# Local and global attention feeding a gated MLP on one core: early loads placed in the line, later return of buffers in the planner, a newly annealed order

## The chip, the cores and the metric

The kernel runs on one core of a Trainium2 chip. The metric is the time of one execution on the device in microseconds (us), as the median of several runs. Engines are named as the profile names them: PE is TensorE's matmul and PEld its weight load, DVE is VectorE, ACT is ScalarE, POOL is GpSimd, SP is SyncE, which here only issues DMA transfers.

## The reference, cut to what matters

There are 8 batches, 8 heads of 64 columns, 512 local and 32 global rows. Local rows attend to a band of 32 neighbours on each side and to the 32 global keys; global rows attend to all 544 keys. The result (576 rows by 512) goes through a gated layer:

```python
s_g = scale * np.matmul(q_g, k_all.transpose(0, 1, 3, 2));  out_g = np.matmul(sm(s_g), v_all)
s_ll = np.where(np.abs(pos[:, None] - pos[None, :]) <= 32, scale * q_l @ k_l.T, -1e9)
out_l = np.matmul(sm(np.concatenate([s_lg, s_ll], -1)), np.concatenate([v_g, v_l], 2))
x = concat(out_g, out_l)                              # [8, 576, 512]
gate = sigmoid(sum_k conv_w[k] * shifted(x, k))       # 5 taps, causal
out = ((gate * (x @ w_val)) @ w_out).astype(float32)
```

Four weight matrices arrive as 64-bit floats, and the kernel splits them into two 32-bit halves itself.

## The kernel before, in words

The work is cut into named steps. A unit `u` (0 to 31) is a pair of heads of a batch, so a batch has four units. For a unit the steps are, in their order of need: `s` (PE, banded scores into the PSUM tiles sx and sy), `mx0`, `mx1` written `mx{u}.0` and `mx{u}.1` (DVE, mask and maximum of a half, which read sx and sy), `exp` (ACT, into the SBUF tile pm), `t` (PE, transposes of pm), `tc` (ACT, copies into pts), `av` (PE, times the values), `norm` (DVE), `xt` (PE, transposes), `xc`, `xh` (ACT), `halo`, `xl` (DVE), and `tap` and `conv` (the gate's taps, on DVE; for the first three units on PE, as `pc` with diagonal matrices that ACT makes in `dg`). For each batch `gs`, `gmax`, `gexp`, `gt`, `gtc`, `gav`, `gnorm`, `gx`, `gxc` do the 32 global rows of all four units, in two halves (`gexp{b}.0` and `gexp{b}.1`). `gs` writes into sx and sy as well, the same two tiles that `s` uses: half 0 is read from sx, half 1 from sy.

When a batch has its units, the layer's steps follow: `sig` (ACT), `g1.b.e.t` (PE, three matmuls each), `gv` (DVE), `gh` (ACT), `gl` (DVE), `g2.b.r.e` (PE, three matmuls each), `ob` (ACT), `st` (ACT, a store). The key `g` instead of a batch stands for the 256 global rows together, which come last. `w{k}.s0` to `w{k}.s7` (DVE) and `w{k}.high` (ACT) split the eight weight pieces; `g1` needs w0 to w3, `g2.0.0.e` needs w4 to w7.

The order of the program is the string `ORDER`, found by annealing outside the kernel. `Plan.order` walks along it, and every engine gets its steps in that order, so each engine executes its own queue strictly in turn. The planner's numbers (costs, `LAG`, `PAIR`, rings of buffers with `take` and `give`) do not put a wait into the program; the real waits come from the tiles that are read and written. They decide which order the annealing thinks good, and how many filler matmuls (`pz`, on zeros) `keep_clock` puts in front of a PE step for which a gap of more than `KEEP` ns is reckoned.

Loads are issued by SP, in order. `transfer` ties each load to the last PE instruction that stands before it in the line, so that the load is issued only when that instruction has ended. The loads named in `FIRST` are issued before the line begins, and wait for nothing on PE; there `q2` is the queries and keys of unit 2, `m0` the mask, `w1` a weight piece and `v0` the values of unit 0.

## Time and profile before

| what | value |
|---|---|
| runs (median, lowest, highest) | 374.15, 373.26, 375.1 us |
| profiled execution: its own time | 373.46 us |
| profiled execution: span from the first to the last instruction | 371.7 us |
| PE busy | 358.6 us |
| DVE busy | 311.6 us |
| ACT busy | 266.8 us |

The profiled execution's own time is 1.8 us longer than its span. Matmuls are pipelined and overlap, so a busy PE also hides short waits.

### The profile page before, as it was taken

Reading aid. Unit: us, or ns where it says so; the run is one execution under the profiler, and the core shown is the slowest. Engines: PE = TensorE matmul, PEld = TensorE weight load, DVE = VectorE, ACT = ScalarE, POOL = GpSimd, SP = SyncE. Lnnn points to the kernel's source line nnn. Section 1 sums busy time; section 2 is a strip of 40 time slices with the busy share of each in tenths; the row PEclk is TensorE's granted clock in tenths of the full one; section 3 lists DMA queues with packets and bytes.
Section 4 is the critical chain, followed back from the end, with each engine's and each line's share of the span. In section 5 each row is a group of like instructions: output and inputs, shape, how many; then the busy total and the mean of one; then the engine's idle time right before and its main releaser. Section 6 shows DMA issues by size and latency. Waiting matters only on the chain.

```text
span 371.7 us, 14822 instructions
## 1 busy us (share of the span) xinstructions
PE 358.6 (96%) x6349; PEld 280.7 (76%) x6349; DVE 311.6 (84%) x1094; ACT 266.8 (72%) x628; POOL 0.9 (0%) x7
## 2 busy tenths in 40 slices
PE   8899999997999899999999999999999999999995
PEld 4665678766878687878878888788778788788894
DVE  4899999998999887998879988888599837986871
ACT  4977869965789488856796777988876696835231
POOL 0000000000000000000000000000000000000000
PEclk9999999999999999999999999999999999999999
DMA  8986886485265733775586244654564110030112
GB/s 289 398 336 198 300 329 195 140 305 188 79 210 239 245 125 119 264 298 177 185 303 239 92 129 176 259 203 160 181 226 156 43 45 30 2 113 31 53 47 72
DMA packets 17250, 66.74 MB, mean 180 GB/s; under 512 B 1952, under 2 KB 4000, under 8 KB 17184
## 3 DMA queue, kind: packets, MB, share of 16 engines
q1 hardware_dynamic: 12240, 57.12, 43.7%
q10 hardware_dynamic: 4944, 8.67, 6.4%
q8 instruction: 50, 0.82, 0.9%
q14 instruction: 16, 0.13, 0.1%
HBM read 56.87 MB, written 8.91 MB: 177 GB/s over the span
## 4 chain that ended last, share of the span: by engine, by line
PE 74%; DVE 19%; ACT 4%; issue 1%; ACTq 0%
PE pv L621 22%; PE po L643 21%; PE ax L514 7%; PE pt L503 6%; PE sx L478 5%; DVE pm L490 3%; PE ax L533 3%; DVE gate L572 2%; PE sy L478 2%; PE ag L446 2%; PE pvg L621 2%; PE pog L643 1%; ACT pm L497 1%; DVE wraw L294 1%; DVE xs L524 1%
## 5 line engine op out<-in xcount | busy, mean ns | idle before, releaser
L497 ACT ACTIVATE pm<-pm,mx 128x128 f32<-128x128 f32 x256 | 81.5, 397 | 14.5 <-DVE mx L490 14.3
L572 DVE SCALAR_TENSOR_TENSOR gate<-xc,cw,gate 128x512 f32<-128x512 f32 x116 | 85.8, 748 | 1.6
L621 PE MATMUL pv<-xh,wvh 128*128 128x512 f32 x128 | 54.7, 428 | 0.6 <-issue 0.6
L643 PE MATMUL po<-woh,gh 128*128 128x512 f32 x128 | 54.3, 424 | 0.0
L621 PE MATMUL pv<-xl,wvh 128*128 128x512 f32 x128 | 50.4, 394 | 0.0
L643 PE MATMUL po<-woh,gl 128*128 128x512 f32 x128 | 50.3, 393 | 0.0
L643 PE MATMUL po<-wol,gh 128*128 128x512 f32 x128 | 50.2, 392 | 0.1
L621 PE MATMUL pv<-xh,wvl 128*128 128x512 f32 x128 | 50.2, 392 | 0.0
L506 ACT COPY pts<-pt 128x512 f32<-128x512 f32 x64 | 36.2, 586 | 19.5 <-PE pt L503 19.3
L478 PE MATMUL sx<-qk 64*32 64x128 f32 x1024 | 38.2, 275 | 3.0 <-ACT pg L420 2.9
L478 PE MATMUL sy<-qk 64*32 64x128 f32 x1024 | 36.9, 275 | 1.1 <-issue 0.7
L514 PEld LDWEIGHTS ax<-v,pts 128*32 128x32 f32 x2048 | 30.7, 109 | 9.2 <-issue 2.8
L503 PE MATMUL pt<-ident,pm 128*128 128x128 f32 x256 | 37.2, 275 | 0.1
L478 PEld LDWEIGHTS sx<-qk 64*32 64x32 f32 x1024 | 28.9, 106 | 10.8 <-ACT pg L420 4.0
L503 PEld LDWEIGHTS pt<-ident,pm 128*128 128x128 f32 x256 | 29.9, 141 | 9.3 <-issue 3.0
L514 PE MATMUL ax<-v,pts 128*32 128x65 f32 x2048 | 35.8, 221 | 0.5 <-ACT xc L537 0.2
L490 DVE CUSTOM_DVE_ANT_0 pm<-sx,mask 128x128 f32<-128x128 f32 x128 | 29.4, 287 | 6.8 <-PE sx L478 6.6
L629 DVE TENSOR_TENSOR gv<-pv,gate 128x512 f32<-128x512 f32 x32 | 22.0, 688 | 8.9 <-PE pv L621 8.8
L649 ACT COPY ob<-po 128x512 f32<-128x512 f32 x32 | 18.7, 586 | 14.9 <-PE po L643 12.6
L490 DVE CUSTOM_DVE_ANT_0 pm<-sy,mask 128x128 f32<-128x128 f32 x128 | 29.4, 286 | 0.0
L537 ACT COPY xc<-ax 128x512 f32<-128x512 f32 x32 | 18.8, 588 | 14.5 <-DVE gate L572 6.0
L621 PEld LDWEIGHTS pv<-xh,wvh 128*128 128x128 f32 x128 | 24.1, 188 | 6.7 <-issue 2.1
(113 smaller groups left out, 660.1 us busy)
## 6 DMA issues: line engine op xcount, KB each, us to landing
v<-in_vw_dram SPq DMA_DIRECT2D x32, 975.0 KB, 5.6
qk<-in_qk_dram SPq DMA_DIRECT2D x32, 624.0 KB, 4.8
out_dram<-ob ACTq DMA_DIRECT2D x32, 256.0 KB, 2.3
wraw<-in_w_val_dram SPq DMA_DIRECT2D x4, 512.0 KB, 12.4
wraw<-in_w_out_dram SPq DMA_DIRECT2D x4, 512.0 KB, 4.8
mask<-in_mask_dram SPq DMA_DIRECT2D x1, 256.0 KB, 4.4
out_dram<-obg SPq DMA_DIRECT2D x4, 64.0 KB, 1.7
out_dram<-obg ACTq DMA_DIRECT2D x4, 64.0 KB, 2.0
```

Source lines behind the costliest of these rows:

```text
L478: on_pe(T.matmul((sx, sy)[h][32 * j:32 * j + 32, i, :], qkt[rows, 32 * m:32 * m + 32], qkt[rows, k0:k0 + P], start=True, stop=True))
L490: V.tensor_tensor_reduce(out=pm[:, h, i, :], in0=s[:, i, :], in1=mask[:, i, :], op0=ALU.add, op1=ALU.min, scale=-SCALE, scalar=3.0e38, acc ...
L497: A.activation(out=pm[:, h, i, :], in_=pm[:, h, i, :], func=AF.Exp, bias=mx[:, c:c + 1], scale=-1.0)
L503: on_pe(T.transpose(pt[:, i, :], pm[:, h, i, :], ident))
L506: A.copy(st[u]["pts"][:, h], st[u]["pt", h])
L514: on_pe(T.matmul(ax[32 * j:32 * j + 32, h, E1 * i:E1 * i + E1], pts[:, h, i, 32 * j:32 * j + 32], vt[:, block_win(4 * i + j), h, :], start ...
L537: A.copy(xc[:, KW - 1:], flat(u)[:, SL:])
L572: V.scalar_tensor_tensor(out=acc, in0=xc[:, k:k + SL], scalar=cw[:, u % NDT, k:k + 1], in1=acc, op0=ALU.mult, op1=ALU.add)
L621: on_pe(T.matmul(box["pv", e], w[:, e, t * P:t * P + P], x, start=(t == 0 and q == 0), stop=(t == NDT - 1 and q == 2)))
L629: V.tensor_tensor(out=box["gv", e], in0=box["pv", e], in1=gates[x0 + e], op=ALU.mult)
L643: on_pe(T.matmul(box["po", r], g[:, e, rs], w[:, e, :], start=(e == 0 and q == 0), stop=(e == NDT - 1 and q == 2)))
L649: A.copy(box["ob", r][:, :at], box["po", r][:, :at])
```

## The change

`FIRST` keeps only three loads: units 0 and 1 of the queries and keys, and the mask. The ten others become steps of the line (`wi0` to `wi3`, `iq2`, `iq3`, `iv0` to `iv3`), and so wait for the PE instruction before them. In the planner, sx and sy of the global scores count as free when both `gexp` halves are done (before: when half 1 is done), and pm counts as free when both `t` halves are done (before: when `tc{u}.1` is done). `KEEP` falls from 1500 to 900, the reckoned cost of `s0` and `s1` rises, and `ORDER` is a new line of the same steps, with the ten loads added.

```diff
 ORDER = """
-cw s0 mx0.0 exp0.0 mx0.1 w0.s0 w0.s1 exp0.1 s1 t0.1 t0.0 w0.s2 w0.s3 mx1.0 tc0.1 w0.s4 tc0.0 w0.s5 av0 mx1.1 dg0 w0.s6
+wi0 cw wi1 dg0 s0 mx0.0 mx0.1 w0.s0 exp0.0 w0.s1 iv0 s1 w0.s2 w1.s0 exp0.1 mx1.0 w1.s1 mx1.1 iq2 w0.s3 iv1 t0.1 t0.0
...
-FIRST = "q0 m0 q1 w0 q2 v0 q3 w1 v1 w2 v2 w3 v3"
+FIRST = "q0 m0 q1"
...
-KEEP = 1500
+KEEP = 900
...
+        elif ("w", k) not in first:
+            plan.add(f"wi{k}", "SP", 450, wraws[k], [f"wi{k - 1}"] if k % 2 and ("w", k - 1) not in first else [])
...
-    for u in range(NQ, NU):
-        plan.add(f"iq{u}", "SP", 450, lambda u=u: load_qk(u), [f"iq{u - 1}"] if u > NQ else [], take=[("qk", u)])
+    for u in range(NU):
+        if ("qk", u) not in first:
+            plan.add(f"iq{u}", "SP", 450, lambda u=u: load_qk(u), [f"iq{u - 1}"] if ("qk", u - 1) not in first else [],
+                     take=[("qk", u)])
...
+        if ("v", u) not in first:
+            plan.add(f"iv{u}", "SP", 450, lambda u=u: load_v(u), [f"iq{u}"] if ("qk", u) not in first else [],
+                     take=[("v", u)])
...
-                     give=[("pt", "gagb"[2 * h:2 * h + 2] + f"{b}")] + ([("s", f"g{b}")] if h else []))
+                     give=[("pt", "gagb"[2 * h:2 * h + 2] + f"{b}")])
...
+        plan.add(f"fs{b}", "FREE", 0, lambda: None, [f"gexp{b}.0", f"gexp{b}.1"], give=[("s", f"g{b}")])
...
-        plan.add(f"s{u}", "PE", 1000, lambda u=u: l_s(u), [f"lq{u}"] + ([f"s{u - 1}"] if u else []),
+        plan.add(f"s{u}", "PE", (1400, 1500)[u] if u < 2 else 1000, lambda u=u: l_s(u), [f"lq{u}"] + ([f"s{u - 1}"] if u else []),
...
-                     give=[("pt", (u, h))] + ([("pm", u)] if h else []))
+                     give=[("pt", (u, h))])
+        plan.add(f"fp{u}", "FREE", 0, lambda: None, [f"t{u}.0", f"t{u}.1"], give=[("pm", u)])
```

The first place is SP at the start of the program: the loads in the order in which they are issued. Before:

```order
L314 DMA qk0_79<-in_qk_dram 128x1248
L843 DMA mask_64<-in_mask_dram 128x512
L314 DMA qk1_82<-in_qk_dram 128x1248
L314 DMA wraw0_84<-in_w_val_dram 128x4x256
L314 DMA qk2_86<-in_qk_dram 128x1248
L314 DMA v0_88<-in_vw_dram 128x1950
L314 DMA qk3_90<-in_qk_dram 128x1248
```

With the change:

```order
L314 DMA qk_79<-in_qk_dram 128x1248
L850 DMA mask<-in_mask_dram 128x512
L314 DMA qk_82<-in_qk_dram 128x1248
L314 DMA wraw_96<-in_w_val_dram 128x4x256 x2
L314 DMA v_166<-in_vw_dram 128x1950
L314 DMA qk_227<-in_qk_dram 128x1248
```

Both pieces of the first weight pair now stand ahead of unit 0's values, and unit 2's queries and keys behind them; all from the weights on wait for PE.

The second place is ACT at the global scores of batch 2, whose exponentials (`pg`) read sx and sy; PE's step `s9` writes the same two tiles next. Before:

```order
L419 ACTIVATE pg2_1_1647<-gs2_2_1_1575,gm2_1_1633 128x160
L420 ACTIVATE pg2_1_1647<-gs1_2_sy_1573,gm2_1_1633 128x384
L565 CAST xh6_1692<-xc6_1593 128x512
L649 COPY ob0_2_1695<-po0_2_1564 128x512
L807 DMA out_0_dram<-ob0_1_1558 128x512
L419 ACTIVATE pg2_0_1718<-gs2_2_0_1574,gm2_0_1629 128x160
L420 ACTIVATE pg2_0_1718<-gs1_2_sx_1572,gm2_0_1629 128x384
```

With the change:

```order
L419 ACTIVATE pg2_0_1619<-gs2_2_0_1556,gm2_0_1608 128x160
L420 ACTIVATE pg2_0_1619<-gs1_2_sx_1554,gm2_0_1608 128x384
L565 CAST xh6_1622<-xc6_1552 128x512
L419 ACTIVATE pg2_1_1647<-gs2_2_1_1557,gm2_1_1613 128x160
L420 ACTIVATE pg2_1_1647<-gs1_2_sy_1555,gm2_1_1613 128x384
L814 DMA out_0_dram<-ob0_1_1617 128x512
```

Half 1 stood first in the queue and half 0 three rows behind it; in the string, `s9` stood between the two. Now both halves stand ahead of `s9`, with one cast between them. Batch 3 (`gexp3.1`, `s13`, `gexp3.0`) changes in the same way.

The third place is DVE at the last step of the last weight piece, `w7.s7` (the row that writes `wol` from `wraw7`), for which `g2.0.0.3` waits. Before:

```order
L294 SCALAR_TENSOR_TENSOR wraw7_1130<-wraw7_1130 128x512
L635 TENSOR_TENSOR gl0_1133<-gv0_2_1321,gh0_1132 128x512
L568 TENSOR_TENSOR xl4_1228<-xc4_1082,xh4_1227 128x512
L288 TENSOR_SCALAR wraw7_1130<-wa7_1222 128x512
L635 TENSOR_TENSOR gl0_1133<-gv0_3_1396,gh0_1132 128x512
L289 SCALAR_TENSOR_TENSOR wol_75<-wraw7_1130 128x512
```

With the change:

```order
L635 TENSOR_TENSOR gl0_1185<-gv0_3_1434,gh0_1184 128x512
L452 TENSOR_SCALAR gd1_1_1463<-ag1_1_1413 128x1
L521 TENSOR_SCALAR mx6_987<-ax6_1245 128x8
L522 RECIPROCAL mx6_987<-mx6_987 128x8
L524 TENSOR_TENSOR xs6_1469<-ax6_1245,mx6_987 128x512
L289 SCALAR_TENSOR_TENSOR wol_75<-wraw7_1066 128x512
```

Of the steps ahead of `w7.s7` on DVE all are the same in both lines, except that `norm6` (three rows) and `mx8.0` (eight rows, further up) now stand ahead of it, and `xl4` behind. On PE the steps ahead of `g2.0.0.3` are the same but for `xt6`, which is now ahead, and `t8.0` in the place of `t7.0`.

## Rows read from the trace of the kernel before

**Rows 1.** The page: busy time of each engine.
```profile
PE 358.6 (96%) x6349; PEld 280.7 (76%) x6349; DVE 311.6 (84%) x1094; ACT 266.8 (72%) x628; POOL 0.9 (0%) x7
```
**Rows 2.** Busy time by stretch, with the view's own column heads.
```profile
core 0: us, PE busy (x) PEld busy (x) DVE busy (x) ACT busy (x) POOL busy (x), PEclk, DMA share, GB/s
5.14:20.00 14.86, 12.90 (x292) 9.02 (x292) 12.93 (x71) 12.17 (x38) 0.00 (x0) 1.00 1.04 399
20.00:80.00 60.00, 58.49 (x1185) 42.00 (x1184) 58.78 (x223) 48.39 (x124) 0.00 (x0) 1.00 0.71 245
80.00:95.00 15.00, 12.95 (x314) 9.90 (x320) 13.66 (x43) 9.15 (x24) 0.00 (x0) 1.00 0.59 217
95.00:125.00 30.00, 30.00 (x575) 23.78 (x576) 29.01 (x103) 23.48 (x56) 0.00 (x0) 1.00 0.58 199
```
**Rows 3.** PE's timeline: start, duration, row [idle before, releaser].
```profile
1.45 3.78 PE L705 MATMUL pz<-zf 128*128 128x512 f32 x4 [1.45 <-DVE zf L844]
...
10.44 2.15 PE L705 MATMUL pz<-zr 128*128 128x512 f32 x7
12.73 1.11 PE L514 MATMUL ax<-v,pts 128*32 128x65 f32 x64
```
**Rows 4.** DVE's timeline at the start: its first weight step, and unit 2's maximum.
```profile
8.63 0.43 DVE L282 TENSOR_SCALAR wa<-wraw 128x512 int32<-128x512 int32 x1 [0.16 <-DMA wraw<-in_w_val_dram]
...
16.09 0.29 DVE L490 CUSTOM_DVE_ANT_0 pm<-sx,mask 128x128 f32<-128x128 f32 x1 [1.05 <-PE sx L478]
```
**Rows 5.** SP's loads: first weight piece, all qk, all v.
```profile
L314 SPq DMA_DIRECT2D wraw<-in_w_val_dram x1: 433/433/433, 2.1 to 2.1; - x1
DMA to landing us min/median/max: 6.5/6.5/6.5
...
L314 SPq DMA_DIRECT2D qk<-in_qk_dram x32: 327/328/1012, 0.7 to 266.1; - x32
...
DMA to landing us min/median/max: 3.6/4.8/11.8
...
L314 SPq DMA_DIRECT2D v<-in_vw_dram x32: 327/328/4680, 3.4 to 280.6; - x32
...
DMA to landing us min/median/max: 4.6/5.6/16.1
```
**Rows 6.** DVE's timeline: a norm, half a mx, an xl, and the last weight step.
```profile
62.13 0.17 DVE L521 TENSOR_SCALAR mx<-ax 128x8 f32<-128x8 f32 x1
...
63.18 0.28 DVE L490 CUSTOM_DVE_ANT_0 pm<-sy,mask 128x128 f32<-128x128 f32 x1
...
64.02 0.69 DVE L294 SCALAR_TENSOR_TENSOR wraw<-wraw 128x512 f32<-128x512 int32 x1
...
73.40 0.69 DVE L568 TENSOR_TENSOR xl<-xc,xh 128x512 fp32r<-128x512 f32 x1
74.00 0.43 DVE L288 TENSOR_SCALAR wraw<-wa 128x512 int32<-128x512 int32 x1
...
75.53 0.68 DVE L289 SCALAR_TENSOR_TENSOR wol<-wraw 128x512 fp32r<-128x512 f32 x1
```
**Rows 7.** PE's timeline around the first matmul that reads wol of the last weight piece.
```profile
75.16 0.63 PE L503 MATMUL pt<-ident,pm 128*128 128x128 f32 x4
...
76.27 0.50 PE L643 MATMUL po<-wol,gh 128*128 128x512 f32 x1
```
**Rows 8.** Timelines: PE at s9 and s13, ACT before s9.
```profile
88.97 0.29 PE L478 MATMUL sx<-qk 64*32 64x128 f32 x1 [1.87 <-ACT pg L420]
...
127.92 0.29 PE L478 MATMUL sx<-qk 64*32 64x128 f32 x1 [1.05 <-ACT pg L420]
...
88.31 0.60 ACT L420 ACTIVATE pg<-gs_sx,gm 128x384 f32<-128x384 f32 x1
```
**Rows 9.** PE's waits, whole span: total us, times, longest.
```profile
PE pv L621 <- issue: 0.6, 1, 0.6
PE gpt L429 <- DVE xg L454: 0.5, 1, 0.5
```

## The prediction

> **What bounds the kernel now.** I read the page first. PE is busy for nearly the whole span, DVE for five sixths of it, ACT for less [rows 1]. The new line holds the same computing steps, so PE's matmuls are the same but for the filler. Nothing can come out of PE's work; the time can only come from PE's waits, or go into new ones. So the question is where PE waits, and what it waits for.

> The windows by stretch answer the first half. From 95 us on PE is busy all the time. In the first 95 us it is not, and there the engine that is never free is DVE: from 5.14 to 20 us it is idle 14.86 - 12.93 = 1.9 us, from 20 to 80 us only 60 - 58.78 = 1.2 us [rows 2]. Beside the attention it splits eight weight pieces in that time. PE's queue runs in step with DVE's, and a step that is put earlier or later in DVE's queue moves the whole program. The place where this is read off is the last step of the last weight piece: DVE starts it at 75.53 us, it takes 0.68, so it ends at 76.21, and PE's first matmul on that half of the weights starts at 76.27 us [rows 6, 7]. After this, PE's own queue is the bound.

> The timelines around PE's longest gaps answer the other half. PE stands 1.87 us before s9 and 1.05 us before s13, both times released by ACT's exponential of the global scores [rows 8]. s9 writes the two PSUM tiles that the exponentials read; the planner took them for free after half 1, while half 0 was queued behind it on ACT. Two smaller gaps remain that are not at the start: 0.6 us before a pv matmul and 0.5 us before a gpt transpose [rows 9].

> **The change part by part.** *The accumulators of the global scores.* In the planner nothing is computed and no wait is added; what counts is that the new line puts both halves of gexp2 ahead of s9, and of gexp3 ahead of s13. The gaps of 1.87 and 1.05 us then go: -2.92 us. At most they go in full, at least nothing of them goes, if s9 then waits for another engine. I take the full value, because the exponential that released s9 began at 88.31 us and PE resumed at 88.97 [rows 8], with no other releaser in sight; how full DVE is there makes a rival below.

> *The probability tiles.* pm now counts as free when both transposes have read it, before: when the copy of half 1 was done. In neither trace row nor gap does a load or a score wait for pm by itself, so this costs and gives nothing at first hand; it only lets the annealing see what is true.

> *The early loads.* Ten loads leave the head of SP's queue and wait for PE. The first of them, a weight piece, now waits for the filler on zf, which ends at 1.45 + 3.78 = 5.23 us [rows 3], where it was issued at 2.1 us before and landed 6.5 us later, 8.6 us [rows 5]. Behind it in SP's queue stand the second weight piece, v0, the queries and keys of unit 2, and everything else, so a late start delays all of them, and DVE's weight steps wait for the first two, PE's av0 for the third. What does a load cost that is issued late? Before, the loads stood in a crowd: DMA engines full at 399 GB/s [rows 2], landings up to 11.8 us for qk and 16.1 us for v, where the quickest took 3.6 and 4.6 us [rows 5]. A weight piece of 512 KB is smaller than a qk load of 624 KB, so with three loads ahead instead of a crowd I estimate 4.0 us, between the quickest qk and the weight piece's own 6.5, and nearer to the first since only qk of unit 1 still moves when it is issued. It lands at 5.23 + 4.0 = 9.2 us. DVE is free for it at 8.63 - 0.16 = 8.47 us [rows 4], so it waits 0.8 us instead of 0.16, with bounds 0.3 (3.6 us) and 3.3 (6.5 us). v0, third in the queue, comes at about the same 12.7 us at which av0 starts now [rows 3], and the copies that av0 needs are no earlier. Against this, DVE's gap of 1.05 us before unit 2's maximum [rows 4] has work to fill it: in the new line norm0 and steps of two weight pieces stand there. Together DVE loses 0.8 us and gains 1.05 + 0.16 = 1.2: 0.4 us earlier by 20 us, with bounds of 0.9 earlier and 2.1 later.

> [...] The rows show early loads landing 11.8 and 16.1 us after their issue, because they queue behind each other, so what the early issue bought was a place in a full queue, and I go by the rows.

> *The filler.* Eleven filler rows of 0.31 us (seven take 2.15 [rows 3]) become four. They stand where PE waits anyway, so by themselves they cost nothing and give nothing. [...]

> *The new line up to w7.s7.* DVE now has norm6 and mx8.0 ahead of that step and xl4 behind it. norm: 63.18 - 62.13 = 1.05 us; half a mx: 64.02 - 63.18 = 0.84; xl: 74.00 - 73.40 = 0.60 [rows 6]. So +1.05 + 0.84 - 0.60 = +1.29 us on DVE; with the 0.4 from the start, w7.s7 ends 0.9 us later, at 77.1 us. PE in turn has one more step behind it at that point, xt6, four transposes, as long as the row that starts at 75.16 and ends with the next start, about 0.5 us [rows 7]. That is work done, not lost. Net, PE's queue is 0.4 us late here, with bounds of 0.1 early and 2.9 late. The steps after it on DVE (mx8.1, gmax2, norm7) are then as far ahead of PE as before.

> *The small gaps.* Of the 0.6 and 0.5 us [rows 9] I take half away, 0.5 us, since a new order keeps some gaps and makes others; bounds 0 and 1.1. Fewer table switches on ACT (the new queue has four loads of the table less) lie in ACT's idle time, which is a quarter of the span.

> *The sum.* -1.87 - 1.05 + 0.4 - 0.5 = -3.0 us. Against the profiled execution's own 373.46 us that gives 370.4 us; against the median of the runs, 374.15, which is 0.7 us more, 371.1 us. I predict the median: **371.1 us**. Over 0.5% (1.9 us) is about what a measurement of this kernel can tell from no change: faster begins below 372.3, slower above 376.0.

> **The rivals.** *DVE takes the wait over.* Once s9 no longer waits for ACT, PE runs into DVE, which is busy 13.66 of 15 us there and 29.01 of the next 30 [rows 2]. For it speaks that DVE's free time up to 125 us is only 1.3 + 1.0 us. Against it: of the 15 us, DVE is idle for 1.34, more than in the 60 us before. The price is the 1.87 us come back: 373.0 us, no change by measure. Chance 0.16.

> *The loads come late (slower).* Place: SP's queue at 5 to 20 us, where each load now follows a PE step. If they take what the first weight piece took, 6.5 us, although the crowd is gone, then DVE waits until 5.23 + 6.5 = 11.7 us, 2.5 us more than in the sum. The queries and keys of unit 3 are asked for only after unit 1's transposes and then come 2.5 us later too, and s3 waits; the weights of the next pair come behind. DVE loses 2.5 us about two times and more: 371.1 + 5.0 = 376.1 us, and each further late load adds to it. It decides from 4.9 us of lost DVE time on. For it: DVE has next to no free time up to 80 us, so each lost us counts. Against: the quickest loads in rows 5. Chance 0.08.

> *PE's clock falls at the start.* [...] The new line has less filler, and PE stands before t0, av0 and av1. The steps from s1 to s3 are some 6 us of matmuls by my estimate (an av is 1.11 us [rows 3], four transposes 0.5 [rows 7]). [...] Against it: the granted clock is 1.00 from 5.14 to 20 us, although PE was not always busy [rows 2]. Chance 0.06. [...]

> *All gaps go.* If the new line also keeps DVE free of its 1.9 us of early idle time and makes no new gaps, the sum is -2.92 - 1.1 + 0.4 - 1.9 = -5.5: 368.6 us. Chance 0.14.

> **How the numbers follow.** My own case has 0.56; its range is 369.4 to 372.9 (small gaps all gone and DVE early, or PE late by 2.2 us). Of it 0.48 lies below 372.3 and 0.08 above. Faster: 0.48 + 0.14 + 0.03 of the first rival = 0.65. Same: 0.08 + 0.13 + 0.06 = 0.27. Slower: 0.08. The range for 8 in 10 leaves out half of the slow rival and the ends of the others: 367.8 to 374.2.

> **What would show it.** Right: no gap before s9 and s13; the first weight step on DVE at about 9.2 us; the last weight step ending at about 77 us; PE without gaps from 95 us on; granted clock 1.00 at the start. Wrong: a first weight step after 11 us, DVE idle more than 4 us between 5 and 80 us, a PE gap of over 1 us released by DVE between 80 and 125 us, or new gaps where half a step is queued behind its user.

## The result, and the profile after

The changed kernel takes 375.29 us in the median of 20 runs (373.79 to 377.54), the kernel before in the same comparison 373.55 (372.69 to 375.1). The ratio is 1.0042, with a 95% interval of 1.0024 to 1.0059: 0.4% slower. That lies inside the 0.5% called no change, but the interval excludes no change, and 371.1 us and the gain were wrong. Below, medians are over all runs of a kernel and ratios leave disturbed runs out; where the two disagree the ratio counts.

The profiled execution took 377.54 us with a span of 375.8, 4.1 us more than the span before. It is the slowest of the 20, so its losses may be larger than those of the median run. First its page: busy time, then PE and the granted clock (PEclk) in 40 slices of 9.4 us, in tenths.

```profile
PE 360.2 (96%) x6342; PEld 282.1 (75%) x6342; DVE 311.4 (83%) x1094; ACT 262.4 (70%) x624; POOL 0.9 (0%) x7
...
PE   7688979999999999999999999999999999999995
...
PEclk9899998999999999999999999999999999999999
```

Then busy time by stretch, as in [rows 2], and six shorter stretches (same columns).

```profile
5.14:20.00 14.86, 10.65 (x280) 7.75 (x264) 11.15 (x58) 9.91 (x31) 0.00 (x0) 0.89 0.80 296
20.00:80.00 60.00, 54.83 (x1153) 38.51 (x1154) 54.63 (x212) 46.00 (x114) 0.00 (x0) 0.97 0.65 227
80.00:95.00 15.00, 15.00 (x224) 11.86 (x223) 14.58 (x47) 10.00 (x26) 0.00 (x0) 1.00 0.88 300
95.00:125.00 30.00, 30.00 (x670) 24.15 (x659) 28.04 (x110) 26.72 (x66) 0.00 (x0) 1.00 0.61 215
...
10.00:15.00 5.00, 2.07 (x37) 1.42 (x40) 4.84 (x25) 3.63 (x13) 0.00 (x0) 0.99 1.01 405
15.00:20.00 5.00, 4.94 (x125) 4.00 (x115) 3.21 (x12) 2.95 (x10) 0.00 (x0) 0.67 0.46 154
50.00:55.00 5.00, 3.09 (x69) 1.61 (x69) 4.93 (x25) 4.25 (x14) 0.00 (x0) 1.00 0.81 271
55.00:60.00 5.00, 4.77 (x19) 3.35 (x20) 4.11 (x13) 1.81 (x4) 0.00 (x0) 0.66 0.53 187
...
56.00:57.00 1.00, 1.00 (x3) 0.56 (x3) 0.94 (x4) 0.94 (x3) 0.00 (x0) 0.50 0.06 16
57.00:58.00 1.00, 1.00 (x3) 0.41 (x2) 0.95 (x3) 0.56 (x2) 0.00 (x0) 0.50 0.50 70
```

From 80 to 125 us PE has no gap: what stood before s9 and s13 [rows 8] is won. It is lost twice over ahead of 80 us. PE idles 14.86 - 10.65 = 4.21 us up to 20 us (before 1.96) and 5.17 from 20 to 80 (before 1.51) [rows 2]. And its work became slower: it is busy 1.6 us longer than before [rows 1] although seven filler rows (2.15 us [rows 3]) are gone, so the same matmuls took some 3.75 us more. Most of that is, by my estimate, the clock: granted at 1.00 in every window of the profiled execution before [rows 2], now two stretches of 3.4 us at 0.50 (14.90 to 18.32 and 55.87 to 59.28 us; last two rows), each behind a gap of PE's. Half of twice 3.4 us is 3.4 us, the most that I let them explain. The sum: +2.25 + 3.66 - 2.05 (80 to 125 us) - 1.05 (s13) + 3.75 - 2.15 = 4.4, against 4.1 us of span.

The timelines of DVE and PE name the places: the first weight piece and av0 as in [rows 3, 4], and the transposes t5.0 and t5.1, where [rows 3] has nothing to set beside.

```profile
9.85 0.43 DVE L282 TENSOR_SCALAR wa<-wraw 128x512 int32<-128x512 int32 x1 [1.54 <-DMA wraw<-in_w_val_dram]
...
11.16 0.47 PE L705 MATMUL pz<-zr 128*128 128x512 f32 x1
14.57 0.73 PE L514 MATMUL ax<-v,pts 128*32 128x65 f32 x28 [2.93 <-ACT pm L497]
...
52.81 0.27 PE L503 MATMUL pt<-ident,pm 128*128 128x128 f32 x1
55.23 1.19 PE L503 MATMUL pt<-ident,pm 128*128 128x128 f32 x7 [2.15 <-ACT pm L497]
```

PE's waits (total, times, longest), and from issue to landing of the first weight piece (issued at 5.04 us), of v0 (6.16 us), and of v0 in the kernel before (3.4 us).

```profile
PE ax L514 <- ACT pm L497: 2.9, 1, 2.9
PE pt L503 <- ACT pm L497: 2.5, 2, 2.1
PE ax L514 <- DMA v<-in_vw_dram: 2.0, 2, 1.8
...
DMA to landing us min/median/max: 4.8/4.8/4.8
...
DMA to landing us min/median/max: 8.3/8.3/8.3
...
DMA to landing us min/median/max: 9.2/9.2/9.2
```

The view puts av0's 2.93 us on an ACT exponential. But v0 lands at 14.44 us, 0.13 before PE goes on, so that wait is v0's; before, it landed at 12.60. The 2.0 us are waits for the third and fifth v. And t5.0's first transpose runs at 52.81, and ACT had ended unit 5's exponentials at 51.70, so the seven that start 2.15 us later are not held by them either; the rows of line 497 that end at 54.63 are unit 6's. What held PE here is the subject of half the experiments.

### The profile page after: what moved, and what is told of

Same layout as the page of the kernel before. It is cut to its first block, busy times and chain, and to the rows that moved or that the text cites. A ratio compares the mean times of both kernels' runs of the same rounds, so it can differ in the third digit from the quotient of the medians.

```text
span 375.8 us, 14813 instructions
## 1 busy us (share of the span) xinstructions
PE 360.2 (96%) x6342; PEld 282.1 (75%) x6342; DVE 311.4 (83%) x1094; ACT 262.4 (70%) x624; POOL 0.9 (0%) x7
## 4 chain that ended last, share of the span: by engine, by line
PE 87%; DMA 5%; DVE 4%; ACT 2%; issue 1%; SPq 0%; ACTq 0%
PE pv L621 24%; PE po L643 24%; PE ax L514 8%; PE pt L503 7%; PE sx L478 5%; DMA v<-in_vw_dram 4%; PE ax L533 3%; PE ag L446 3%; PE sy L478 2%; PE pc L597 2%; DMA wraw<-in_w_val_dram 2%; PE pvg L621 2%; PE pog L643 1%; PE gpt L426 1%; PE gs_sx L403 1%; ACT pm L497 1%
## 5 line engine op out<-in xcount | busy, mean ns | idle before, releaser
L497 ACT ACTIVATE pm<-pm,mx 128x128 f32<-128x128 f32 x256 | 80.3, 395 | 7.1 <-DVE mx L490 6.9
L503 PE MATMUL pt<-ident,pm 128*128 128x128 f32 x256 | 38.8, 280 | 2.5 <-ACT pm L497 2.5
L503 PEld LDWEIGHTS pt<-ident,pm 128*128 128x128 f32 x256 | 31.3, 144 | 11.6 <-ACT pm L497 4.2
L643 PEld LDWEIGHTS po<-woh,gh 128*128 128x128 f32 x128 | 24.1, 188 | 6.7 <-issue 1.8
```

What stands on the lines that cost most here:

```text
L497: A.activation(out=pm[:, h, i, :], in_=pm[:, h, i, :], func=AF.Exp, bias=mx[:, c:c + 1], scale=-1.0)
L503: on_pe(T.transpose(pt[:, i, :], pm[:, h, i, :], ident))
L643: on_pe(T.matmul(box["po", r], g[:, e, rs], w[:, e, :], start=(e == 0 and q == 0), stop=(e == NDT - 1 and q == 2)))
```

## The experiments

Four theories. **L**: the ten early loads wait for PE, come late, and PE waits for v. **C**: less filler lets PE's clock fall. **O**: the order of the early work loses by itself. **P**, added when the traces showed gaps without a fitting releaser: PE runs out of its own program, which comes in pieces while it runs. The page of the changed kernel lists a queue (q8 of the kind "instruction", first row: 50 packets, 0.82 MB, so 16 KB each), and the view of DMA from 52.7 to 53.95 us, over the gap at t5, has one of its packets (second row; the trace has it from 52.81 to 53.91). That these are PE's instructions is my inference, and what each holds an estimate from these counts: 0.82 MB over PE's 12,684 matmuls and weight loads is 65 bytes for each, and 12,684 over 50 packets is 254, or 127 matmuls with their loads.

```profile
q8 instruction: 50, 0.82, 0.9%
...
q8 instruction: 1, 0.02, 5.5%
```

**1. Loads free.** Changed line, loads issued at once.

```
-FIRST = "q0 m0 q1"
+FIRST = "q0 m0 q1 w0 w1 v0 q2 v1 q3 w2 w3 v2 v3"
-wi0 cw wi1 dg0 s0 mx0.0 ... iv0 s1 ... iq2 w0.s3 iv1 ... iq3 s2 ... wi2 ... wi3 s3 ... iv2 w3.s1 iv3
+cw dg0 s0 mx0.0 ... s1 ... w0.s3 ... s2 ... s3 ... w3.s1
```

> The changed kernel, with the ten early loads taken out of the line and issued at once before it, in the same sequence (w0 w1 v0 q2 v1 q3 w2 w3 v2 v3); the line of work and the four filler rows stay. Theory L (the loads that wait for PE arrive late, and DVE and PE wait for them): the first v lands near 12.6 us as in the kernel before instead of 14.44, DVE's waits for weight pieces (1.54 and 0.87) fall under 0.3, PE's wait for the third v (1.8) goes; about 4 us less than the changed kernel's 375.3, so 371 to 372. Theory C (PE's clock falls after its waits, since less filler stands there): the filler is the same, so the time follows the clock: over 374 if rows at the lower level remain. Theory O (the new order of the early work is itself worse): within 1 us of 375.3.

Measured 373.86 us, ratio 1.0002 (0.9979 to 1.0025). Every wait that L names went (v0 landed at 12.60), but only about 0.4% came back: more than O allows and less than L forecast. PE now stood in front of s3:

```profile
22.17 0.42 PE L478 MATMUL sx<-qk 64*32 64x128 f32 x1 [3.08 <-DVE wraw L288]
...
20.00:30.00 10.00, 7.83 (x86) 5.15 (x87) 6.99 (x30) 5.36 (x18) 0.00 (x0) 0.66 0.72 268
```

Scores read no weight, so the releaser named is only the last event; the fourth qk had landed at 19.11. The clock was 0.66 over the ten us from 20. This execution took 375.87 us, 2 us above the median of 1; it also waited 1.81 us for a v at 297.91 us, far behind the start.

**2. More filler.**

```
-                if not opened and gap > KEEP:
-                    keep_clock(int((gap - 400) * 0.55 / 235))
+                if t.name in {'s1': 4, 'av0': 7}:
+                    keep_clock({'s1': 4, 'av0': 7}[t.name])
```

> The changed kernel with the filler rows of the kernel before: 4 rows ahead of the second scores and 7 ahead of the first product with v, in place of 3 and 1. Theory C (the clock): the stretch at half clock after the first wait (3.4 us, up to 1.7 us of work lost) does not come, the mean clock is 0.995 or more, 373.6 to 374.2. Theories L (loads late) and O (order worse): the filler lies inside PE's wait of 2.9 us for the first v, and the time stays at 375.3 within 0.5.

Measured 377.31 us, ratio 1.0054 (1.0022 to 1.0086): nothing gained. The stretch at 0.50 behind av0 went, another came around a later wait, of 1.71 us for the fourth qk, at 22 us (the clock is 0.97 over the first 51.65 us, in a row further down). More filler removed one fall of the clock, and the time did not follow.

**3. The global exponentials alone.** Kernel before, two tasks moved.

```
-gexp2.1 conv5.2 g2.0.3.0 s9 ... gexp2.0 ... gexp3.1 ... s13 gexp3.0
+gexp2.1 gexp2.0 conv5.2 g2.0.3.0 s9 ... gexp3.1 gexp3.0 ... s13
```

> The kernel before with two tasks moved in its line: the late halves of the global exponentials of batches 2 and 3 stand directly behind the early halves, ahead of the local scores s9 and s13; nothing else changes. If the middle term of the prediction is right: PE's waits of 1.87 and 1.05 us behind them go, 2.9 us less than 373.55, 370.6 to 371.2. If another wait takes their place (DVE's or ScalarE's next task comes late by as much): 372.5 to 373.6.

Measured 371.54 us, ratio 0.9932 (0.9911 to 0.9953): 2.5 us won where 2.92 were forecast. The gap before s13 is gone, that before s9 has shrunk from 1.87 to this:

```profile
87.75 0.29 PE L478 MATMUL sx<-qk 64*32 64x128 f32 x1 [0.86 <-ACT pg L420]
```

**4. Hybrid.** The line and `FIRST` of the kernel before for 279 tasks (up to s8), then the remaining tasks in the changed line's order.

> The line of the kernel before for its first 279 tasks (up to s8, near 68 us; early loads and 11 filler rows as there), then the rest of the changed kernel's line. If the loss lies wholly in the start and the gain wholly behind it (theories L, C and O alike, against the rival that the changed line's later part loses too): 373.55 less the 3.9 us that the traces show as won behind the start, so 369.2 to 370.4. If the later part is no better by itself: 372.5 to 374.

Measured 370.89 us, ratio 0.9918 (0.9895 to 0.9940), clock 1.00, half a microsecond above the forecast. So the loss lies in the start (the changed start stands at 1.0042 with the same rest) and the gain behind it.

**5. Hybrid with the waits.** Ten loads put into the hybrid's line.

```
-FIRST = "q0 m0 q1 w0 q2 v0 q3 w1 v1 w2 v2 w3 v3"
+FIRST = "q0 m0 q1"
+wi0 wi1 cw s0 iv0 ... s1 iq2 iv1 ... s2 iq3 ... xt0 wi2 ... pc0.0 iv2 iv3 ... av1 wi3
```

> The hybrid of the fourth experiment (start of the kernel before, then the changed line; 370.89 us), with one edit: the ten early loads wait for PE at the changed kernel's places. Theory L (the waits themselves cost the start): the first v lands about 1.8 us later, and with the later weight pieces and v tiles it loses 1.5 to 3 us: 372.4 to 374. Theory O (the order of the early work is what loses): within 0.6 of 370.9.

Measured 375.34 us, ratio 1.0053 (1.0036 to 1.0069). The waits alone cost 4.4 us on the old order by the medians and 5.0 by the ratios, above L's own range. PE waited for v0 and then for the third qk, and its clock fell (0.89 from 5.14 to 20 us):

```profile
14.91 1.12 PE L514 MATMUL ax<-v,pts 128*32 128x65 f32 x64 [2.14 <-DMA v<-in_vw_dram]
16.99 0.39 PE L478 MATMUL sx<-qk 64*32 64x128 f32 x1 [0.96 <-DMA qk<-in_qk_dram]
```

**6. Two loads later.** Changed kernel, `iq7 iv5` moved to behind `t5.1`.

> The changed kernel (375.29 us) with two loads, q7 and v5 (issued at 46.63 and 48.35 us in its trace), moved behind the transposes t5.1, some 4 us later; all else stays. Theory P (PE stood still from 53.09 to 55.23 because the next 16 KB of its own program, fetched from 52.81 to 53.91, had stood behind these loads' packets): the fetch comes by 50 us, that gap goes, and with it the clock's fall behind it (1.3 us): 2 to 3.5 us less, 371.8 to 373.3. If the gap has another cause (ScalarE's exponentials, as the view of waits names it): the gap stays, 374.6 to 376.

Measured 376.40 us, ratio 1.0065 (1.0044 to 1.0086): a miss in time. The gap at t5 and the clock's fall behind it did go, the q8 packet coming at 50.45 in place of 52.81 us; but v5, now late itself, held av5 for 1.3 us, and in this execution PE waited 3.4 us for v0. The step was right and the trade bad.

**7 and 9. Hybrid up to s3.** The line before only for the first 22 us, without the third weight's pieces.

> The line of the kernel before only up to the scores s3 (near 22 us, without the pieces of the third weight), all early loads issued at once, and the changed line from there. If the changed order loses nothing by itself after 22 us (theory L: its loads came late there): within 0.7 of the hybrid, 370.6 to 371.6. If the order from 22 to 57 us loses by itself, or PE's program comes late there as in theory P: 373 to 375.5, with a PE gap of about 2 us near 50 us.

> As the run before it was meant, with the third weight now issued ahead of the fourth again: the line of the kernel before up to the scores s3 (near 22 us, without the third weight's pieces), all early loads issued at once, 11 filler rows, and the changed line from there. If the changed order loses nothing by itself behind 22 us: within 0.7 of the hybrid's 370.9. Theory P (PE's own program comes late near 50 us, where products with v, scores and short transposes stand close together) or O (the order from 22 to 57 us loses): 372.5 to 375, with a PE gap of about 2 us near 50 us for P.

The first, 379.15 us (ratio 1.0166), says nothing of the order: issued ahead of the third weight piece, the fourth goes into the buffer half of the second, which is then computed from wrong data, and DVE waited 4.30 us for it. In the second (w2 ahead of w3) the ratio is 1.0015 (0.9991 to 1.0040), 1% above the hybrid, with a gap inside s6 at 50.93 us of 1.75 us and one of 1.55 us for DVE at 34.56 us (0.67 in the hybrid), although its trace (373.22 us) is of its fastest execution. So the changed order from 22 to 57 us loses by itself, as P and O would have it.

**8. v0 ahead of the third qk** in the hybrid.

> The hybrid (370.89 us) with the first v issued ahead of the third qk, and 3 filler rows in place of 7 ahead of the first product with v. Its PE waited 2.26 us there for that v, which landed at 12.6: it should land near 11.0, and 1.0 to 1.6 us less come of it, 369.3 to 369.9. Rival: the third qk lands 2.4 us later (12.6 in place of 10.2) and scores s2 or ScalarE's copies take the wait over: 370.6 to 371.2.

Measured 371.29 us, ratio 0.9933 (0.9920 to 0.9946): the rival came true. The 2.26 us of the expectation were mostly filler: in the hybrid's trace the filler ends at 12.43 us and av0 starts at 12.73. Here v0 landed at 11.12 and av0 began at 11.40, but the third qk landed only at 12.69, and PE stood still three times before and inside s2, the longest 0.58 us at 14.63.

**10. Convolution earlier.** As 1, with `pc0.0 pc0.1` ahead of `av1`.

> The first experiment (changed line, early loads issued at once, 373.86 us) with two convolution steps, pc0.0 and pc0.1, moved ahead of the product with v av1, where the kernel before has them. In the first experiment PE stood still for 3.08 us ahead of the scores s3 with the piece of its program landing inside the gap, and its clock fell behind it. Theory P (the changed order takes up PE's program faster than the pieces come while the loads fill the queues; rows of 512 columns stretch it): the gap falls under 0.6 and the fall with its 2.8 us goes, 369.5 to 371.5. If the gap is a load's (the fourth qk): the gap stays, and 373.5 to 374.5.

Measured 373.67 us, ratio 0.9988 (0.9968 to 1.0009). PE waited 2.35 us for the halo, a DVE row of 0.06 us that stands behind steps of two weight pieces. This wait is of O's kind, and the run no test of P.

**11. Three loads free.** `FIRST = "q0 m0 q1 w0 w1 v0"`, seven loads left in the line.

> The changed kernel (375.29 us) with three of the ten early loads, w0, w1 and the first v, issued at once; the other seven wait in the line as before. Theory L: the first v lands at 12.6 in place of 14.44 and DVE's wait for the first weight goes, 1.5 to 2.5 us less; the wait of 1.78 for the third v stays: 372.8 to 373.8. If all ten must be free (PE's wait moves on to the fourth qk or the third v): 374.7 to 375.5.

Measured 373.20 us, ratio 0.9980 (0.9962 to 0.9999): 0.6% below the changed kernel, as L has it; 2.3 us of wait for the third v stayed, and 1.70 us stood before s3.

**12 and 13. Pairs parted.** As 9 with `pc2.2` between `av4` and `s6`; as 1 with `pc0.0 pc0.1` between `av1` and `s3`.

> The run of the hybrid up to s3 (375.91 us; PE gap of 1.75 us inside the scores s6, near 50 us) with one convolution step, pc2.2, moved from behind s6 to between the product with v av4 and s6. Theory P: four rows of 512 columns (0.9 us) give the piece of PE's program time to come; the gap falls to under 0.9 and 1 to 2 us come off: 374 to 375. If the gap is not of the program: it stays at 1.7 or moves whole, within 0.6 of 375.9.

> The first experiment (changed line, early loads at once, 373.86 us; PE gap of 3.08 us ahead of s3, clock fall of 6.8 us behind it) with the convolution steps pc0.0 and pc0.1 moved to between av1 and s3, where DVE's halo they need is ready. Theory P: the 1.9 us of convolution lie inside the wait, the gap falls to about 1.2, the fall is shorter or goes: 370.8 to 372.3. If the wait is one of s3's own operands: nothing is won, 373.3 to 374.5.

12: 374.41 us, ratio 1.0019 (0.9993 to 1.0046), by ratio no change from 9, though the gap fell from 1.75 to 0.87, by the 0.9 us of convolution put ahead of it. 13: 376.00 us, ratio 1.0060 (1.0036 to 1.0084), a miss by time, and the most telling one. The gap did not shrink and did not stay with s3; it now stood before pc0.0, whose halo (first row below) was there at 19.42:

```profile
19.36 0.06 DVE L542 MEMSET xc<- 128x4 f32 x1
...
22.04 0.59 PE L597 MATMUL pc<-xc,diag 128*128 128x512 f32 x1 [3.00 <-DVE wraw L288]
```

In these two runs it is the place in the program that counts, matmul 349, and not the task. The windows from the span's start to just before the gap count PE's matmuls. At s3 in 1 and at pc0.0 in 13:

```profile
0.00:22.15 22.15, 15.18 (x348) 9.65 (x348) 15.97 (x79) 15.71 (x44) 0.85 (x7) 0.98 0.95 350
...
0.00:22.00 22.00, 14.83 (x348) 9.56 (x349) 16.09 (x79) 15.71 (x44) 0.85 (x7) 1.00 0.95 349
```

And near 50 us, at t5 in the changed kernel, inside s6 in 2 and in 9 (both with seven filler rows more, so that the same count comes at an earlier task):

```profile
0.00:55.20 55.20, 44.40 (x984) 28.32 (x984) 45.49 (x203) 39.91 (x110) 0.85 (x7) 0.97 0.77 275
...
0.00:51.65 51.65, 43.64 (x984) 28.50 (x984) 41.94 (x182) 37.36 (x102) 0.85 (x7) 0.97 0.80 280
...
0.00:50.90 50.90, 43.45 (x984) 27.22 (x984) 42.59 (x182) 37.35 (x102) 0.85 (x7) 1.00 0.79 284
```

In each of these, PE starts its next matmul a nearly fixed time, 1.28 to 1.45 us, after the end of the q8 packet that the trace shows there. In the table the larger differences belong to places without such a wait (no gap there is over 0.4 us):

| kernel | matmul 349: packet ends, starts | matmul 985: packet ends, starts |
|---|---|---|
| before | 20.20, 21.45 (+1.25) | 47.93, 54.30 (+6.4) |
| hybrid (4) | 19.30, 20.98 (+1.68) | 47.74, 54.02 (+6.3) |
| changed | 17.93, 22.14 (+4.2) | 53.91, 55.23 (+1.32) |
| 1, loads free | 20.73, 22.17 (+1.45) | 52.65, 53.94 (+1.29) |
| 2, more filler | 18.01, 20.07 (+2.1) | 50.40, 51.68 (+1.28) |
| 9, hybrid to s3 | 19.45, 21.03 (+1.58) | 49.61, 50.93 (+1.32) |
| 13, pair parted | 20.68, 22.04 (+1.37) | 55.05, 56.35 (+1.31) |

**14. Repaired.** As 11, with both partings and v2, v3 issued earlier.

> The run with three free loads (373.2 us) with three edits: pc0.0 and pc0.1 between av1 and s3, pc2.2 between av4 and s6, and the third and fourth v issued directly behind the fourth and fifth weight pieces, before their old places. Theories L and P together: PE's gaps of 1.70 (ahead of s3) and 2.29 us (for the third v) go, and the clock's fall behind the second: 3.5 to 4.5 us less, 368.7 to 369.9. If DVE's order is what remains (theory O): a wait for a maximum, a halo or a weight piece takes their place, 371.5 to 373.

Measured 375.53 us, ratio 1.0041 (1.0018 to 1.0063): neither. The wait for the third v went, and at matmul 985 no gap was left; but at matmul 349 PE stood 2.46 us in front of pc0.0, and its clock was at 0.66 from 20 to 30 us. As in 13, the task moved to that count stood still there.

One piece of the estimated 127 ahead of matmul 349 stands matmul 222 (349 - 127). There the kernel before itself has a gap, inside s2, for which the view names no releaser ("issue"):

```profile
14.93 0.30 PE L478 MATMUL sy<-qk 64*32 64x128 f32 x2 [0.73 <-issue]
```

The first q8 packet ends at 13.51, 1.42 us earlier. Gaps of 0.28 to 0.80 us stand at matmul 222 in 3, 4, 7, 8, 9, 12 and 15 too, 1.22 to 1.45 us behind that packet. So, if P holds, it already cost the old order a little, and in 8, where matmul 222 came at 14.63 us (14.48 in the hybrid), it helped to take back what the earlier v0 had won.

**15. Hybrid with less filler.** As 4, with 3 and 1 rows.

> The hybrid (370.89 us, 11 filler rows, no stretch at half clock) with the filler of the changed kernel: 3 and 1 rows. Theory C (less filler alone lets PE's clock fall, since PE then stands idle for 2 us ahead of the first product with v): a fall of 3.4 us near 12 to 17 us and 1 to 1.7 us more, 371.9 to 372.6. If filler alone is worth nothing, as the prediction has it: 370.5 to 371.3, mean clock 0.998 or more.

Measured 370.59 us, ratio 0.9915 (0.9896 to 0.9934), clock 1.00 from 5.14 to 125 us, although PE stood 1.74 us in front of av0:

```profile
10.98 0.47 PE L705 MATMUL pz<-zr 128*128 128x512 f32 x1
13.20 1.01 PE L514 MATMUL ax<-v,pts 128*32 128x65 f32 x57 [1.74 <-DMA v<-in_vw_dram]
```

C is refuted on the old order with its loads free: the filler is worth nothing there. This hybrid and 4, level with each other, are faster than both kernels of the case.

## Why the prediction was wrong, step by step

- *The accumulators, -2.92 us*: the mechanism was right and the size nearly so; alone it measured -2.5 us by the ratio (experiment 3), with 0.86 us left before s9. In the changed line nothing of either gap is left.
- *The early loads*: the step that failed. Its first half was mis-sized: the first weight piece took 4.8 us and not 4.0, and DVE waited 1.54 and not 0.8. Its second half was wrong in kind. v0 "at about the same 12.7 us" came at 14.44, since it was issued 2.8 us later and still took 8.3 us; and later loads (third and fifth v) held PE too. I let each lateness count through DVE alone, and charged it 0.8 us, which DVE's gap before unit 2's maximum was to give back. That gap did not close; it grew from 1.05 to 1.62 us (row below), since s2 on PE came late. On the old order the waits cost 4.4 us (experiment 5). Issuing early had the better sign here: the long landings in a crowd [rows 5] cost PE only 0.30 us at av0 in the hybrid, where the pieces needed first stand first.
- *The filler, nothing*: right (experiments 2 and 15).
- *The small gaps, -0.5 us*: about right. Neither gap of [rows 9] is in the changed trace, and one of 0.55 us for a v stands at 298.99 us.
- *The line up to w7.s7*: forecast to end at 77.1 us, it ended at 82.61 + 0.68 = 83.29, 7.1 us later than before, and PE's first matmul on that half (line 643) came at 83.47, 7.2 us later and again right behind. The extra work on DVE was sized well: it was busy 1.0 us longer up to that row (1.29 forecast). The other 6.1 us are DVE's idle time, for the most part four waits: for the first weight piece and unit 2's maximum, as above, 0.87 us for another weight piece, and 3.01 us for the global scores of batch 1, which PE wrote late. So PE's lateness came back to PE through DVE; the sum had +0.4 us for all of this, beside half a microsecond of work for xt6.

```profile
19.41 0.29 DVE L490 CUSTOM_DVE_ANT_0 pm<-sx,mask 128x128 f32<-128x128 f32 x1 [1.62 <-PE sx L478]
...
62.33 0.56 DVE L410 TENSOR_REDUCE gm<-gs_sx 128x1 f32<-128x384 f32 x1 [3.01 <-PE gs_sx L403]
...
82.61 0.68 DVE L289 SCALAR_TENSOR_TENSOR wol<-wraw 128x512 fp32r<-128x512 f32 x1
...
83.47 0.40 PE L643 MATMUL po<-wol,gh 128*128 128x512 f32 x1
```

- *The rivals*: "the loads come late" is what happened, at 0.08, and its 376.1 us is close to 375.29, in part by luck, since its path went through DVE alone and the real one through PE as well, with the gap at matmul 985 beside it. "PE's clock falls" also happened, behind the waits and, by experiments 2 and 15, not for the missing filler. No run shows less filler alone lowering the clock, for which the 0.06 stands: experiment 15, with 3 and 1 rows, has 1.00 from 5.14 to 125 us. Nor do the filler rows of 0.95 and 0.31 us [rows 3] show a slower PE, since the kernel declares the two fillers with different types (`zf` F32, `zr` F32R). What the runs show is eight transposes in 1.97 us at a granted 0.50 (16.21 us in the changed kernel) and in 1.03 at 1.00 (122.89). "DVE takes the wait over" and "All gaps go" did not happen.
- *Not in the prediction at all*: the gaps that P puts down to PE's own program. Without any load waiting, the new early order, with its own sequence of loads, stands at 1.0002 where the old stands at 0.9918, 3.1 us (experiments 1 and 4). In the trace of 1 the gap of 3.08 us at matmul 349 and the clock's fall around it are its largest loss; what the order of DVE's steps adds (the halo of experiment 10) was not measured by itself. The losses do not add: the waits cost 4.4 us on the old order, but about 1.5 on the new one (1.0042 against 1.0002), and the packet times suggest why: with waiting loads the packet reckoned to matmul 349 came earlier (it ended at 17.93, not 20.73).
- *Open*: what delays a packet. The traces show what changed: the packet for matmul 985 starts 3.9 us after PE's 858th matmul, one piece ahead, in the changed kernel and 2.4 us after it in the kernel before, but PE takes the 127 matmuls between in 2.4 to 4.1 us wherever the new order runs there and in 8.8 to 9.7 us on the old. In none of the 17 traces does a packet start more than 148 matmuls ahead of the one that it is reckoned to bring (127 apart, from 222 on). That a packet stands behind loads' packets is only argued from experiment 6, where moving two loads brought it 2.4 us sooner; how the queues share the engines was not shown.

## What to carry to other kernels

Judge a load by when its data is needed first, not by how long it is under way: in the kernel before, where a crowd is issued in the order of need, one v took 16.1 us from issue to landing [rows 5] and the view of PE's waits names no load, while in experiment 5 a v0 of 7.9 us that had waited for its turn cost PE 2.14. When a gap's named releaser does not feed the waiting instruction, count the engine's instructions up to the gap in two variants of the kernel; here the same counts, 349 and 985, under different tasks pointed to the program itself. Where a change joins a reordering and a rule for loads, run the old start with the new rest first: it showed in one run that a gain and a loss had been packed together.

## What the hardware showed that was not expected

The granted clock fell to 0.50 for 3.4 us behind PE's gaps of 2.93 and 2.15 us in the changed kernel and for 6.8 us around the 3.08 us of experiment 1 (0.66 from 20 to 30 us), and did not fall behind the 1.87 us before s9 [rows 8], with 1.00 from 80 to 95 us [rows 2], or the 1.74 us of experiment 15, with 1.00 from 5.14 to 125 us. In these runs the length of the gap alone does not decide: in experiment 2 the clock fell around one of 1.71 us. So a wait of PE in the start cost more than its own length here, by my estimate up to 1.7 us of work for each stretch of 3.4 us at 0.50. The kernel before is not free of it either: of its 20 executions beside experiments 1 to 4, 7 have a mean granted clock of 0.993 to 0.995 and take 374.2 to 376.2 us, the other 13 have 0.997 to 1.000 and take 373.0 to 374.1. Of the changed kernel's 20, all lie between 0.988 and 0.995.
